# A third group of block 2 turned by VectorE, the last chunk's store in halves, and a new instruction order

## The chip, the cores and the metric

The kernel runs on one core of one Trainium2 chip. Its time is the device time of one execution in microseconds; the median over several runs is compared.

## The reference

Attention with a local window and block summaries, followed by a two-layer block with the gate h * cos(h):

```python
# q, k, v: (4, 8, 768, 64); block 32, window 16; w_in (512, 2048), w_out (2048, 512)
k_sum = k.reshape(B, H, nb, 32, D).max(axis=3)        # 24 block summaries per head
v_sum = v.reshape(B, H, nb, 32, D).mean(axis=3)
scores_l = where(|i - j| < 16, q @ k.T / sqrt(D), -1e9)
scores_s = q @ k_sum.T / sqrt(D) + log(32)
a = softmax(concat([scores_l, scores_s]))             # with + 1e-9 in the denominator
x = (a @ concat([v, v_sum])) -> (3072 tokens, 512)
h = x @ w_in
out = (h * cos(h)) @ w_out
```

The weights arrive as 64-bit floats, the rest as 32-bit floats, and the result is 32-bit.

## The kernel before

The 3072 tokens are eight blocks of 384 (two per batch). In a block, attention works in four **groups** a to d, one for each pair of heads; a name such as b2 is group b (the second pair) of block 2. A group has six tiles of 64 queries. Each tile sees 96 keys and 24 summaries, so its probabilities are 120 wide, padded to 128 with one column for the 1e-9.

The steps of a group, by their names in the order list: `q`, `k`, `v`, `m` load queries, keys, values and the value summaries (one line each on SP's queue of DMAs); `tq`, `tk` turn q and k by TensorE (lines 502, 515) and `cq`, `ck` copy the turned tiles out of PSUM; `ks` takes the block maxima of k (VectorE, line 536); `sc` are the scores (TensorE, line 569); `z` scales and masks (line 580); `mx`, `su`, `ex`, `sm`, `iv`, `nm` are the maximum (VectorE), its subtraction (GpSimd), exp (ScalarE), the sums (VectorE), their inverse (VectorE) and the normalization (GpSimd, line 617); `tp` and `cp` turn the probabilities by TensorE and copy them out; `va` multiplies with the values (TensorE, line 670); `xh` and `xl` split the result into a high and a low part (fp32r).

There is a second way to turn. Two strings of 32 digits, one digit per group, choose it: `TURNS = (q and k, probabilities)`. With a 1, q and k are loaded as 32x32 squares (four DMAs each, line 450, where the other way has two, line 456), and VectorE turns 32x32 elements at once (`qt` line 520, `kt` line 525, straight into the place where TensorE reads them). The probabilities are turned by VectorE too (`pt`, line 640), then written to DRAM (`po`, line 648) and fetched back in four DMAs in another order of the squares (`pi`, line 655), because a transpose of squares leaves the squares where they were. Before the change the groups c2, d2 and all of the blocks 3 to 7 are turned that way, and the blocks 0 and 1 and the groups a2 and b2 by TensorE.

The two-layer part goes in 128 **steps** s0 to s127: for one block and one of 16 slices of 128 of the hidden width, `up` is 12 matmuls of 128x384 (line 714: x high and low with the weight's high, x high with its low part), then `tu`, `re`, `si`, `sq`, `ga` make h * cos(h) by ScalarE and VectorE in turn (lines 724 to 739), `hi` and `lo` split it, and `dh`, `dl` are 6 and 3 matmuls of 128x512 (line 770) into three accumulators, one per chunk of 128 tokens. At the end of a block `ta` takes the three chunks out of PSUM with the sign turned (line 803 on ScalarE, 805 on VectorE) and `st` stores them (line 810). The blocks come in this order: the first six slices of block 0 with part results put away, all of block 1, the rest of block 0, then the blocks 2 to 7.

The **slices** of the weights, w0 to w15, are converted once from 64 bits: `l` loads 1 MB in two DMAs, `ab` (ScalarE), `cl`, `sh`, `lb`, `fb` (VectorE, lines 393, 399, 407, 415) put the bits together, and `hi`, `lo` split into high and low part. The **value summaries** v0_0, v0_1 and so on are loaded (`l`), halved (`h`) and summed (`s`).

All engines run in program order, and that order is written out by hand: the string ORDER is a list of 2247 tokens `who.what.arguments`, where digits are PSUM banks or staging buffers and a last letter the engine (a ScalarE, v VectorE, p GpSimd). The kernel is built by walking the list, so on each engine and on SP's queue the instructions stand as in the list; semaphores order the engines against each other. An instruction that waits holds all that stands behind it on its engine, a DMA on SP's queue too.

Of the kernel before, what the change touches and what calls it, by code (L numbers as in the profile page):

```python
# [20 lines left out]
TURNS = ("00000000001111111111111111111111", "00000000001111111111111111111111")  # L21
# [6 lines left out]
b0.k a0.q a0.k c0.q d0.k b0.tk.0.0 c0.k b0.ck.0.a a0.tq.1 b0.tk.1.2 a0.cq.a v0_1.l b0.ks.1 a0.tk.0.3 b0.ks.0 v0_0.l  # L28
a0.tk.1.4 a0.ck.0.a a0.ks.0 a0.ms.5.6 a0.ck.1.a a0.ks.1 b0.q a0.sc a0.z.1.a a0.z.0.v w1.l a0.mx c0.tk.0.7 a0.su
d0.tk.0.1 c0.ck.0.a d0.tk.1.0 d0.q d0.ks.0 c0.tk.1.3 d0.ck.0.a c0.tq.4 c0.ks.0 c0.ck.1.a c0.ms.6.5 v0_1.h.p d0.ks.1  # L30
c0.cq.a d0.ck.1.v a0.ex w0.l c0.ks.1 c0.sc v0_0.h.v c1.q b0.tq.1 c0.z.1.a b0.ms.7.4 a0.sm b0.ck.1.a v0_0.s.p b0.cq.a
v0_1.s.v c0.z.0.a b0.sc a0.v w1.ab.0 c0.mx w2.l d0.tq.0 b0.z.1.a d0.ms.3.5 w1.cl c0.su b0.z.0.a a0.iv d0.cq.a
w1.sh.6.7 d0.sc a0.nm c0.ex w1.lb c0.m d0.z.0.a d0.z.1.a a0.tp.0.2 w1.fb.1 w0.ab.0 a0.tp.1.1 a0.m d0.mx a0.cp.1.a w5.l
a0.cp.0.a w0.cl d0.su w1.hi.a c0.sm c0.v w0.sh.4.5 w1.lo.p d0.ex d0.m w0.lb w2.ab.0 a0.va.0 c0.iv b1.q w2.cl c0.nm
w0.fb.1 w3.l w2.sh.6.7 w0.hi.a c0.tp.0.3 c0.tp.1.1 a0.xh.a a1.m w0.lo.p d0.sm c0.cp.1.a w5.ab.0 w2.lb d1.m b1.tq.2
c0.cp.0.a d0.iv w5.cl d0.nm c0.va.1 a1.q w2.fb.1 w4.l w5.sh.4.5 w2.hi.a d0.tp.0.3 d0.tp.1.6 d0.v c0.xh.a w2.lo.p b0.mx
w3.ab.0 w5.lb c1.m a1.tq.7 d0.cp.1.a d0.cp.0.a c0.xl b0.su d1.q a1.cq.a a1.ms.6.3 w5.fb.1 b0.ex a1.sc w3.cl d1.v
w5.hi.a b0.sm c1.tq.1 b1.cq.a w3.sh.4.5 w5.lo.p d0.va.7 b0.m a1.z.0.a a1.z.1.a c1.ms.2.6 b0.iv w3.lb d0.xh.a c1.v
w4.ab.0 b0.nm a0.xl c1.cq.a b0.v a1.mx c1.sc w4.cl a1.su a1.v b0.tp.0.3 d0.xl c1.z.0.a w4.sh.0.1 b0.tp.1.7 c1.z.1.a
# [3 lines left out]
w8.sh.6.7 c1.nm a1.va.2 w10.l s1.re w3.hi.a c1.tp.0.0 d1.z.0.v w8.lb c1.tp.1.4 d1.z.1.a w3.lo.p s0.sq s2.up.5 s1.si
d1.mx c1.cp.0.a s0.ga s1.sq d1.su a1.xh.v s0.hi.a s3.up.0 w8.fb.0 c1.cp.1.a w9.ab.1 s0.lo.p s1.ga s2.tu c1.va.3 w9.cl
d1.ex s1.hi.v a2.tq.4 w8.hi.v s1.lo.p s0.dh.6.7.1 b2.q s2.re a1.xl w6.l w8.lo.p s0.dl s3.tu a2.cq.v s2.si d1.sm s1.dh
b2.v s3.re s1.dl d1.iv c1.xh.v d1.nm s3.si s4.up.4 s2.sq c1.xl s3.sq s2.ga w7.ab.0 w9.sh.2.3 d1.tp.0.5 s2.hi.a w7.cl
b1.ex s2.dh s2.lo.p s3.ga w9.lb v1_0.s.p d1.tp.1.0 s4.tu b1.sm d1.cp.1.a s3.hi.a s4.re s5.up.0 v1_1.l d1.cp.0.a b1.iv
w9.fb.1 b1.nm s4.si w7.sh.2.3 s3.lo.p d1.va.5 s4.sq s2.dl w9.hi.v s5.tu s3.dh d1.xh.a s4.ga w9.lo.p w10.ab.0 d1.xl
s5.re b1.tp.0.4 w7.lb s5.si b1.tp.1.5 s3.dl s4.hi.a v1_1.s.p s5.sq s4.dh w7.fb.1 b1.cp.0.a b1.cp.1.a s5.ga w7.hi.a
b1.va.4 v1_2.l s4.lo.v w12.l w10.cl s5.hi.a s4.dl w7.lo.p b1.xh.a s5.dh b1.xl w10.sh.2.3 s6.up.5 w10.lb v1_2.s.p  # L50
w10.fb.0 s7.up.0 s6.tu w6.ab.1 s5.lo.p v1_3.l s6.re w10.hi.v s5.dl s7.tu w6.cl w10.lo.p s8.up.4 s6.si s7.re s5.ta.1.a
s7.si s5.st.1 v1_3.s.v s6.sq s9.up.7 s7.sq s6.ga s5.ta.2.a v1_4.l s7.ga s6.hi.a w6.sh.2.3 s7.hi.a s6.lo.p s10.up.5
s5.ta.0.a s7.lo.p s8.tu s5.st.0 w6.lb w12.ab.0 s5.st.2 v1_4.s.p s6.dh.1.0.6 s8.re w6.fb.1 s8.si s8.sq s6.dl v1_5.l
s8.ga w6.hi.a s7.dh w11.l w12.cl s9.tu w6.lo.p a2.v s7.dl s8.hi.a s9.re s11.up.4 w12.sh.2.3 s9.si s9.sq b2.m s9.ga
s8.lo.p w12.lb s12.up.7 a2.m v1_5.s.p s10.tu s9.hi.a s10.re w12.fb.0 s10.si s8.dh w11.ab.1 s9.lo.p v1_6.l w15.l
w12.hi.a w11.cl s8.dl s9.dh w11.sh.2.3 s10.sq w12.lo.p s11.tu s10.ga s9.dl s11.re s10.hi.a s13.up.5 w11.lb s11.si
s10.lo.p s11.sq v1_6.s.p s11.ga s12.tu s10.dh w11.fb.0 s11.hi.a w15.ab.1 s12.re s10.dl w13.l w15.cl s12.si s14.up.4
# [126 lines left out]
def tile_kernel(  # L184
# [177 lines left out]
    class Slice:  # L362
# [27 lines left out]
        def clamp(self):  # L390

            uf = self.u.bitcast(F32)
            nc.vector.tensor_scalar(out=uf, in0=uf, scalar1=W_LO, scalar2=W_HI, op0=ALU.max, op1=ALU.min)
# [308 lines left out]
    class Step:  # L702
# [88 lines left out]
        def take(self, i, *args):  # L791
# [142 lines left out]
```

## Time and profile before

| | |
|---|---|
| median of 3 runs | 661.95 us (660.78 to 662.87) |
| the profiled execution | 662.1 us |
| its span, first to last instruction | 660.2 us |
| TensorE matmuls busy | 633.9 us, 96% of the span |
| VectorE busy | 451.1 us, 68% |
| ScalarE busy | 366.2 us, 55% |
| GpSimd busy | 214.6 us, 33% |
| DMA | 72.68 MB, mean 110 GB/s |
| mean granted TensorE clock | 0.987 |

The span is the profiler's time from the first to the last instruction; the execution's time has 1.9 us more around it. A busy engine may still be off the path that sets the end. PEld is TensorE's weight load, which overlaps its matmuls. SPq rows are the times at which SP's queue issues a DMA, not the transfer itself.

### The profile page before, as it was taken

How to read it: one execution, taken by the hardware profiler on the slowest of the kernel's cores; microseconds unless marked ns; L12 is line 12 of the kernel's file. 1: busy time of each engine (PE TensorE's matmuls, PEld its weight loads, DVE VectorE, ACT ScalarE, POOL GpSimd, SP SyncE). 2: the span in 40 equal slices, each digit the busy share in tenths (PEclk: the TensorE clock that was granted, in tenths of full speed). 3: DMA queues.
4: the chain of work that ended last, by engine and by line, in shares of the span. 5: the costliest groups of instructions: out<-in, count | busy, mean ns of one | idle time of the engine just before them, and what ended most of it. 6: DMA issues, size and time to landing. Idle time of an engine off the chain costs nothing.

```text
span 660.2 us, 13296 instructions
## 1 busy us (share of the span) xinstructions
PE 633.9 (96%) x5150; PEld 561.5 (85%) x5150; DVE 451.1 (68%) x792; ACT 366.2 (55%) x645; POOL 214.6 (33%) x217
## 2 busy tenths in 40 slices
PE   6569999999999999999999999999999999999997
PEld 4347889889888989898988988989898988989996
DVE  3998998988656676658786667577686564534433
ACT  3666968776663375546575663335545554443443
POOL 4674777754220242302333340012332132010001
PEclk9879999999999999999999999999999999999999
DMA  9898725443331443434553544423243424000001
GB/s 229 260 268 224 239 94 176 160 111 59 69 108 52 128 127 105 115 71 98 123 156 78 150 125 132 92 54 81 85 120 104 104 91 115 0 1 17 32 1 48
DMA packets 164647, 72.68 MB, mean 110 GB/s; under 512 B 134441, under 2 KB 153193, under 8 KB 164585
## 3 DMA queue, kind: packets, MB, share of 16 engines
q1 hardware_dynamic: 164584, 71.84, 40.6%
q8 instruction: 40, 0.66, 0.4%
q14 instruction: 23, 0.18, 0.1%
HBM read 53.72 MB, written 15.73 MB: 105 GB/s over the span
## 4 chain that ended last, share of the span: by engine, by line
PE 87%; SPq 4%; DMA 4%; ACT 2%; issue 1%; DVE 1%; POOL 1%; ACTq 0%
PE banks L770 40%; PE banks L714 39%; PE banks L569 4%; PE banks L670 3%; DMA late<-in_moe_w_out_dram 3%; SPq L456 1%; SPq L493 1%; SPq L477 1%; ACT stage L388 1%; ACT L732 0%; POOL w L356 0%; SPq L485 0%; PE banks L626 0%; ACT w L350 0%; SPq L254 0%
## 5 line engine op out<-in xcount | busy, mean ns | idle before, releaser
L714 PE MATMUL banks<-xh,w 128*128 128x384 f32 x1024 | 271.8, 337 | 1.1 <-ACT pt L350 0.7
L770 PE MATMUL banks<-w,gh 128*128 128x512 f32 x768 | 199.1, 394 | 0.0
L714 PEld LDWEIGHTS banks<-xh,w 128*128 128x128 f32 x1024 | 185.9, 188 | 3.9 <-ACT pt L350 0.9
L714 PE MATMUL banks<-xl,w 128*128 128x384 f32 x512 | 171.4, 335 | 0.0
L770 PEld LDWEIGHTS banks<-w,gh 128*128 128x128 f32 x768 | 142.0, 188 | 29.0
L356 POOL TENSOR_TENSOR gl<-t,gh 128x384 fp32r<-128x384 f32 x57 | 58.5, 1027 | 242.9 <-DVE gh L352 86.0
L724 ACT ACTIVATE t<-banks 128x384 int32<-128x384 f32 x128 | 62.2, 489 | 131.1 <-DVE gl L356 56.1
L727 DVE SCALAR_TENSOR_TENSOR t<-t,banks 128x384 f32<-128x384 int32 x128 | 69.5, 547 | 61.2 <-ACT t L724 60.7
L770 PE MATMUL banks<-w,gl 128*128 128x512 f32 x384 | 109.6, 393 | 0.0
L739 DVE SCALAR_TENSOR_TENSOR t<-t,banks 128x384 f32<-128x384 f32 x128 | 69.8, 547 | 45.4 <-ACT t L735 44.9
L732 ACT ACTIVATE t<-t 128x384 f32<-128x384 f32 x128 | 66.3, 523 | 60.1 <-DVE t L727 59.4
L714 PEld LDWEIGHTS banks<-xl,w 128*128 128x128 f32 x512 | 96.1, 188 | 1.7
L770 PEld LDWEIGHTS banks<-w,gl 128*128 128x128 f32 x384 | 71.3, 188 | 14.8 <-POOL gl L356 0.2
L593 POOL TENSOR_TENSOR sc<-sc,m 128x720 f32<-128x720 f32 x28 | 39.5, 1410 | 88.9 <-DVE m L588 83.8
L735 ACT ACTIVATE t<-t 128x384 f32<-128x384 f32 x128 | 65.9, 522 | 2.4
L617 POOL TENSOR_TENSOR sc<-sc,r 128x720 f32<-128x720 f32 x28 | 39.6, 1416 | 73.1 <-DVE r L614 70.2
L350 ACT CAST gh<-t 128x384 fp32r<-128x384 f32 x71 | 36.2, 510 | 41.3 <-PE banks L770 21.8
L356 DVE TENSOR_TENSOR gl<-t,gh 128x384 fp32r<-128x384 f32 x71 | 40.6, 573 | 19.6 <-PE banks L770 12.0
L356 POOL TENSOR_TENSOR w<-stage,w 128x1024 fp32r<-128x1024 f32 x15 | 36.7, 2448 | 14.7 <-ACT w L350 12.8
L569 PEld LDWEIGHTS banks<-kd,qd 64*64 64x64 f32 x1344 | 27.8, 133 | 9.6 <-issue 5.3
L580 DVE SCALAR_TENSOR_TENSOR sc<-banks,mask 128x360 f32<-128x360 f32 x48 | 24.7, 523 | 16.5 <-PE banks L569 16.3
L569 PE MATMUL banks<-kd,qd 64*64 64x96 f32 (+1 forms) x1344 | 30.9, 231 | 0.6 <-ACT qd L508 0.4
(100 smaller groups left out, 606.8 us busy)
## 6 DMA issues: line engine op xcount, KB each, us to landing
pd<-stage SPq DMA_DIRECT2D x22, 384.0 KB
late<-in_moe_w_in_dram SPq DMA_DIRECT2D x16, 512.0 KB
late<-in_moe_w_out_dram SPq DMA_DIRECT2D x16, 512.0 KB
pt<-pd SPq DMA_DIRECT2D x66, 96.0 KB
vn<-in_v_dram SPq DMA_DIRECT2D x52, 120.0 KB
out_dram<-stage SPq DMA_DIRECT2D x23, 256.0 KB
kn<-in_v_dram SPq DMA_DIRECT2D x24, 192.0 KB
qn<-in_q_dram SPq DMA_DIRECT2D x88, 48.0 KB
```

The source lines that it names most:

```text
L350: eng.copy(out=out, in_=in_)
L356: eng.tensor_tensor(out=lo, in0=src, in1=hi.bitcast(F32), op=ALU.subtract)
L569: nc.tensor.matmul(out=self.sp[hh][s * QT : (s + 1) * QT, c, lo : lo + n], lhsT=self.qd[rows, t * QT : (t + 1) * QT], rhs=self.kd[rows, ke ...
L593: nc.gpsimd.tensor_tensor(out=self.sc, in0=self.sc, in1=self.m.unsqueeze(2).broadcast_to([P, U, NK]), op=ALU.subtract)
L617: nc.gpsimd.tensor_tensor(out=self.sc, in0=self.sc, in1=self.r.unsqueeze(2).broadcast_to([P, U, NK]), op=ALU.mult)
L714: nc.tensor.matmul(out=self.h, lhsT=w_of(name, self.f)[:, c * P : (c + 1) * P], rhs=x_of(self.blk, part, c), start=n == 0, stop=n == last,)
L724: nc.scalar.activation(out=self.t.bitcast(I32), in_=self.h, func=AF.Copy, scale=1.0 / TWO_PI)
L727: nc.vector.scalar_tensor_tensor(out=self.t, in0=self.t.bitcast(I32), scalar=-TWO_PI, in1=self.h, op0=ALU.mult, op1=ALU.add)
L732: nc.scalar.activation(out=self.t, in_=self.t, func=AF.Sin, scale=0.5)
L735: nc.scalar.activation(out=self.t, in_=self.t, func=AF.Square, scale=math.sqrt(2.0))
L739: nc.vector.scalar_tensor_tensor(out=self.t, in0=self.t, scalar=-1.0, in1=self.h, op0=ALU.add, op1=ALU.mult)
L770: nc.tensor.matmul(out=self.acc[i], lhsT=g[:, i * P : (i + 1) * P], rhs=w_of(name, self.f), start=self.first and n == 0, stop=self.last an ...
```

## The change

`TURNS` gets a 1 for b2 in both strings, so b2 is turned by VectorE as c2 and d2 are: its q and k come in squares, its `tq`, `cq`, `tk`, `ck`, `tp`, `cp` go, and `qt`, `kt`, `pt`, `po`, `pi` come. The clamp of a weight slice (`cl`) can go to GpSimd too, and does for w3 and w7. The last chunk of the last step is taken out of PSUM in two halves of 256 columns, the first by ScalarE (`ta`), the second by VectorE (`tb`), and stored by two DMAs (`st`, `sb`). The whole order list is written anew (2245 tokens, different from the first token on), with other banks and staging buffers and with some operations on another engine.

```diff
-TURNS = ("00000000001111111111111111111111", "00000000001111111111111111111111")
+TURNS = ("00000000011111111111111111111111", "00000000011111111111111111111111")
...
-b0.k a0.q a0.k c0.q d0.k b0.tk.0.0 c0.k b0.ck.0.a a0.tq.1 b0.tk.1.2 a0.cq.a v0_1.l b0.ks.1 a0.tk.0.3 b0.ks.0 v0_0.l
+a0.q b0.k a0.k c0.k a0.tq.0 d0.k c0.q b0.tk.0.1 b0.tk.1.2 b0.ck.0.v v0_0.l b0.ks.0 a0.tk.0.3 a0.tk.1.4 a0.ck.0.a
...
-s127.lo.p s127.dh s127.dl s127.ta.1.1.a s127.ta.0.0.v s127.ta.2.a s127.st.1 s127.st.2 s127.st.0
...
+s127.si s127.sq s127.dl s127.ga s126.dh s127.hi.a s127.lo.p s126.dl s127.dh s127.dl s127.ta.2.a s127.ta.1.1.v
+s127.st.2 s127.ta.0.0.v s127.st.1 s127.tb.2.v s127.st.0 s127.sb.2
...
-        def clamp(self):
+        def clamp(self, eng):
...
-            nc.vector.tensor_scalar(out=uf, in0=uf, scalar1=W_LO, scalar2=W_HI, op0=ALU.max, op1=ALU.min)
+            eng.tensor_scalar(out=uf, in0=uf, scalar1=W_LO, scalar2=W_HI, op0=ALU.max, op1=ALU.min)
...
+        def negative(self, eng, to, from_):
+            if eng is nc.scalar:
+                eng.mul(out=to, in_=from_, mul=-1.0)
+            else:
+                eng.tensor_scalar_mul(to, from_, -1.0)
+
+        def take_half(self, i, h, eng):
+            if (i, 0) not in self.o:
+                t = xp.tile([P, 2, TB], F32R, name="last", tag="xh0%d" % (self.blk % 2)).rearrange("p c n -> p (c n)")
+                self.o[i, 0], self.o[i, 1] = (t[:, n * DM // 2 : (n + 1) * DM // 2].bitcast(F32) for n in range(2))
+            self.negative(eng, self.o[i, h], self.acc[i][:, h * DM // 2 : (h + 1) * DM // 2])
...
+        def store_half(self, i, h):
+            r0, c = self.blk * TB + i * P, slice(h * DM // 2, (h + 1) * DM // 2)
+            nc.sync.dma_start(out=out[r0 : r0 + P, c], in_=self.o[i, h])
```

In the new list's front, v0_1's halving is on VectorE instead of GpSimd, b0's first and a0's second half of turned keys are copied by VectorE and d0's second by ScalarE, `a0.iv` stands ahead of `w1.cl`, `w4.lb` and `a1.sm` stand behind `b0.xl`, SP's queue has d0.v and b0.v ahead of w4's load and further forward, and a0.v behind c0.m and a0.m. Where b2 is turned, the list reads:

```text
b2.kt.0 s18.si a2.iv w14.lo.v a2.nm s17.dl b2.kt.1 s20.up.5 s18.sq b2.qt c2.k s19.tu s18.ga b2.ks.0 s18.hi.a
a2.tp.0.2 b2.ks.1 s18.lo.p c2.q b2.sc.3.0
...
b2.pt.0 s21.ta.0.1.a b2.po d2.sc.7.3
...
s22.dh.4.7.3 s23.lo.p s24.re a2.xl b2.pi d2.su s25.tu
...
c2.sm s22.dl s24.si s23.dh c2.iv s25.re c2.nm s28.up.6 s24.sq s25.si s24.ga s24.hi.a s24.lo.v b2.va.0
```

More of the change, by code (lines that the diff above doesn't have):

```diff
@@ L43 @@
[L43 to L47, printed above, removed]
@@ L893, in tile_kernel @@
             up="up", tu="turns", re="residue", si="sine", sq="square", ga="gate", hi="high_part",
[L894 removed]
+            lo="low_part", dh="down", dl="down_low", fe="fetch", ad="add", ta="take", tb="take_rest", st="store",
+            sb="store_rest",
         ),
```

306 lines of the change are left out of this document (157 added, 149 removed).

## Prediction

> **What bounds the kernel now.** I read the page's busy times and slices first, then the busy times by stretch, then who waits for whom. The page:
>
> ```profile
> PE 633.9 (96%) x5150; PEld 561.5 (85%) x5150; DVE 451.1 (68%) x792; ACT 366.2 (55%) x645; POOL 214.6 (33%) x217
> PE   6569999999999999999999999999999999999997
> ```
>
> TensorE is busy for 633.9 of 660.2 us, and its gaps lie in the first slices and the last. The stretches show where (columns: stretch, its length, busy us and instruction counts of PE, PEld, DVE, ACT and POOL, granted clock, DMA share, GB/s):
>
> ```profile
> 20.00:30.00 10.00, 4.01 (x82) 2.82 (x75) 9.50 (x11) 6.89 (x11) 5.44 (x7) 0.91 0.89 259
> 30.00:40.00 10.00, 5.06 (x53) 4.20 (x55) 9.89 (x13) 5.18 (x7) 8.96 (x5) 0.50 0.90 265
> 40.00:50.00 10.00, 6.86 (x99) 5.25 (x96) 9.64 (x13) 6.97 (x12) 7.11 (x5) 0.84 0.88 231
> 60.00:80.00 20.00, 19.12 (x184) 16.65 (x183) 18.05 (x29) 17.68 (x30) 12.73 (x9) 1.00 0.86 269
> 140.00:180.00 40.00, 40.00 (x411) 36.25 (x406) 31.59 (x54) 26.72 (x47) 17.52 (x13) 1.00 0.31 58
> ```
>
> There are three stages. From 20 to 50 us VectorE is nearly full (9.50, 9.89, 9.64 of 10), the DMA engines carry about 0.9, and TensorE is half idle. From about 100 us TensorE has no gap (nines in all slices but the last, 40.00 of 40 from 140 to 180). At the end, stores alone remain. So a matmul taken away after 100 us is worth its own time, an engine that gets faster there is worth nothing, and in the front what counts is when VectorE and the loads deliver. TensorE's waits, in us, times, longest:
>
> ```profile
> PE banks L670 <- ACT late L606: 4.9, 1, 4.9
> PE banks L670 <- DMA x<-in_v_dram: 2.2, 1, 2.2
> PE banks L626 <- POOL late L617: 2.2, 2, 1.7
> PE banks L714 <- ACT pt L350: 0.7, 1, 0.7
> ```
>
> **Term 1: b2's turns leave TensorE, -1.6 us.** b2 loses 15 transposes by TensorE: three for q, six for k, six for the probabilities. Their cost is the time from their first start to the start of the next matmul:
>
> ```profile
> 140.58 0.55 PE L502 MATMUL banks<-ident,qn 128*128 128x128 f32 x3
> 140.88 0.48 PE L770 MATMUL banks<-w,gh 128*128 128x512 f32 x1
> ...
> 146.52 0.82 PE L515 MATMUL banks<-ident,kn 128*128 128x128 f32 x6
> 147.10 0.48 PE L770 MATMUL banks<-w,gl 128*128 128x512 f32 x1
> ...
> 174.72 0.82 PE L626 MATMUL banks<-ident,sc 128*120 128x128 f32 x6
> 175.47 1.09 PE L569 MATMUL banks<-kd,qd 64*64 64x96 f32 x48
> ```
>
> That is 0.30 + 0.58 + 0.75 = 1.63 us, all inside the stretch without gaps. In their place VectorE gets one q, two k and one probability transpose:
>
> ```profile
> L640 DVE STREAM_TRANSPOSE stage<-sc 128x768 f32<-128x768 f32 x22 | 21.4, 973 | 7.8 <-POOL sc L617 6.9 <-DMA out_dram<-stage 0.9
> L525 DVE STREAM_TRANSPOSE kd<-kn 128x384 f32<-128x384 f32 x20 | 11.4, 569 | 0.0
> ```
>
> q and each half of k are 128x384, so 3 x 0.57 + 0.97 = 2.7 us, in a stretch in which it is idle for 40 - 31.59 = 8.4 us. I cost it at nothing. If that cover were gone, the step residues and gates behind them on VectorE would be 2.7 us late, and a later up would hold TensorE by at most that. ScalarE loses five copies out of PSUM less one that VectorE did.
>
> On SP's queue b2's loads become four of q and four of k where there were two of each, and the probabilities go out and come back through DRAM. The same things as other groups issue them:
>
> ```profile
> 155.72 2.02 SPq L450 DMA_DIRECT2D kn<-in_k_dram  x4
> 161.60 1.85 SPq L450 DMA_DIRECT2D qn<-in_q_dram  x4
> 185.70 0.34 SPq L648 DMA_DIRECT2D pd<-stage  x1
> 188.40 1.72 SPq L655 DMA_DIRECT2D pt<-pd  x4
> ```
>
> That is 2.0 + 1.9 + 0.3 + 1.7 = 5.9 us of issue, less some 2 us that the old loads took. SP has room, since the DMA share is 0.31. From the store at 185.70 to the end of the fetches' issue at 190.1 are 4.4 us. In the new order 87 matmuls stand between b2.po and b2.va (one group's scores, two ups, two downs less one low part); at 40.00 us for 411 from 140 to 180 these are 8.5 us, so the way through DRAM is covered. c2.k, which needs the one key buffer that b2.kt.1 frees, stands 72 matmuls or 7 us ahead of c2.kt.0 and takes 2.0 us to issue.
>
> [...]
>
> **Term 2: the new order in the front, -1.6 us.** I multiplied VectorE's instructions in both order lists by the mean durations below and compared what stands ahead of the first step's matmuls (s0.up, at 58.27 us, which waits for b0.xl).
>
> ```profile
> L407 DVE SCALAR_TENSOR_TENSOR banks<-late,banks 128x1024 int32<-128x1024 int32 x16 | 19.6, 1224 | 0.2
> L393 DVE TENSOR_SCALAR stage<-stage 128x1024 f32<-128x1024 f32 x16 | 12.9, 809 | 4.3 <-ACT stage L388 4.1
> L609 DVE TENSOR_REDUCE r<-sc 128x6 f32<-128x726 f32 x28 | 25.0, 896 | 3.3 <-ACT sc L606 3.1
> ...
> 17.16 1.38 DVE L259 TENSOR_TENSOR late<-late 96x1024 f32<-96x1024 f32 x1 [1.16 <-DMA late<-in_v_dram]
> 22.61 1.65 DVE L393 TENSOR_SCALAR stage<-stage 128x1024 f32<-128x1024 f32 x1 [0.37 <-ACT stage L388]
> 57.57 0.56 DVE L356 TENSOR_TENSOR xl<-banks,xh 128x384 fp32r<-128x384 f32 x1
> ...
> 58.27 0.43 PE L714 MATMUL banks<-xh,w 128*128 128x384 f32 x1
> ```
>
> Ahead of w1.cl (22.61) the new list gives VectorE one halving of v more (1.38), net one copy (0.55, by L356's row) and a0.iv (a reciprocal of 128x6, some 0.2 as the smallest of all here): 2.1 us. VectorE waits 1.16 + 0.37 us there, so some 0.6 us of it shows. Between w1.cl and b0.xl (57.57) the lists differ by four instructions that are no longer there: w3.cl (0.81, now POOL's), w4.lb (1.22) and a1.sm (0.90), now behind, and a0.iv (0.2), now ahead: 3.1 us. VectorE is full there, so b0.xl could come 3.1 - 0.6 = 2.5 us sooner. The moved work comes due later: up to s6.up five instructions have left (a0.iv 0.2, w3.cl and w7.cl 0.8 each, one copy 0.55, one weight cast of about 1.0, between the rows of 0.81 and 1.22 for its size) and three have come (two casts of a step, some 0.4 each, as 3/8 of the weight cast's elements, and w10.lb, 1.22): 3.3 - 2.0 - 0.6 leaves 0.7 us sooner. TensorE then runs no further ahead than VectorE allows, so the gain lies between 0.7 and 2.5, and I take the middle, 1.6.
>
> The loads must let it. In the old order d0.v stood behind w4's 1 MB and landed for 48.33, where TensorE had waited 2.2 us (the L670 row above); now it stands ahead of w4. b0.v too is five loads further ahead. Against that, a0.v now comes last of its group on SP, behind c0.m and a0.m:
>
> ```profile
> 31.65 1.67 PE L670 MATMUL banks<-pt,vn 120*64 120x64 f32 x24 [4.89 <-ACT late L606]
> ```
>
> Its three DMAs at some 0.5 us of issue each (0.46, a quarter of L450's 1.85 for four) are 1.5 us, so a0.va, which starts at 31.65, may start some 1.6 us later. The next group of probabilities on TensorE waits 1.7 us anyway (longest of POOL late L617), which hides it. If this cover is gone and VectorE gains nothing, the front is 1.6 us later. Ends of this term: -2.5 and +1.6.
>
> **Term 3: the last chunk in halves, +0.4 us.** The end now:
>
> ```profile
> 655.18 0.69 DVE L805 TENSOR_SCALAR stage<-banks 128x512 f32<-128x512 f32 x1 [2.07 <-PE banks L770]
> 655.40 0.60 ACT L803 ACTIVATE stage<-banks 128x512 f32<-128x512 f32 x1 [3.35 <-PE banks L770]
> 655.66 0.39 PE L770 MATMUL banks<-w,gl 128*128 128x512 f32 x1
> 656.03 0.33 SPq L810 DMA_DIRECT2D out_dram<-stage  x1
> 656.08 0.60 ACT L803 ACTIVATE last<-banks 128x512 f32<-128x512 f32 x1
> 656.71 0.33 SPq L810 DMA_DIRECT2D out_dram<-last  x1
> 657.13 0.41 SPq L810 DMA_DIRECT2D out_dram<-stage  x1
> ...
> 657.00:658.00 1.00, 0.00 (x0) 0.00 (x0) 0.00 (x0) 0.00 (x0) 0.00 (x0) 1.00 1.04 389
> 658.00:659.00 1.00, 0.00 (x0) 0.00 (x0) 0.00 (x0) 0.00 (x0) 0.00 (x0) 1.00 0.91 350
> ```
>
> ScalarE's half ends at about 656.08 + 0.4 = 656.48 (between 0.60 for the whole and 0.30 for half of it). On SP this half now stands first, so the other two stores, the first of which was ready at 656.03, wait for it: SP starts 0.45 us later. On VectorE chunks 1 and 0 take 2 x 0.69 from 655.40, to 656.78, and the second half some 0.4 more, to 657.2; SP, with four issues of 0.33 to 0.41, starts its last at about 657.6 where it was 657.13, +0.5. The DMA engines are full from 657 to 659 (1.04, 0.91), so the same bytes started 0.45 us later end that much later. A last store of half the bytes gives back up to half of 256 KB at 389 GB/s, 0.3 us. So +0.15 to +0.5; I take 0.4. Below nothing, -0.3, only if the fewer bytes count in full and the later start not at all.
>
> **The sum.** -1.6 - 1.6 + 0.4 = -2.8 us. The profiled execution took 662.1 us (660.2 of span, 1.9 around it), 0.15 above the median of the runs, 661.95. So the profiled time becomes 659.3 and the median 659.15, say 659.2. The rest of the new order I cost at nothing: after 100 us TensorE waits for nobody, and the mean number of other steps' matmuls between a step's up and its down, counted in the two lists from step 6 on, grows from 64 to 70, so the steps keep a little more reserve.
>
> **The rivals.** *The front gives everything back*: VectorE's 0.7 us by s6.up is small, and a wait of TensorE for w3 or the conversions after it eats it. For it speaks that VectorE is nearly full at 60 to 80 us too (18.05 of 20); against it, that TensorE waits so little there (0.7 for ACT pt). Then 661.95 - 1.6 + 0.4 = 660.75.
>
> *The half clock spreads, slower than before.* The clock is at 0.50 from 30 to 40 us, after a stretch in which TensorE did 4.01 of 10 us. If a0.va's wait of 4.9 us grows by the 1.6 of a0.v, the clock may stay down through the next stretch as well. The 6.86 busy us of 40 to 50 would then take up to twice as long; half of that, 3.4 us, I count, because part of it already runs at less than full clock (0.84). With the 1.6: 661.95 - 1.6 + 0.4 + 3.4 + 1.6 = 665.75. It decides where TensorE does no more than some 5 of 10 us from 40 to 50 as well. Against it stands the shorter wait for d0.v. [...]
>
> *The turned group holds TensorE, so that the saving doesn't show.* b2.sc stands right behind b2.ks.1 with no matmul between. So it did before (b2.ks.0) and TensorE did not wait, but the new order has three transposes of 0.57 us packed ahead of it. TensorE waiting there for as long as it saves, with the front's gain: 661.95 - 1.6 + 0.4 = 660.75.
>
> **The chances.** The forecast 0.60 (own range 657.6 to 661), the front given back 0.18, the half clock 0.13, the held group 0.09. A measurement tells 0.3%, 2.0 us, from no change, so faster means below 659.96: three quarters of the forecast's 0.60, 0.45, and a little of the others. The two middle rivals and the rest of the forecast are no change: 0.40. Slower has the half clock and a little more: 0.15. The range goes from 656.8 (front -2.5, tail -0.3, and half a microsecond for the unknown) to 663.2, with the slower case beyond it.
>
> **What would show it.** Right: TensorE instructions fall by 15 transposes and nothing is idle on it from 100 us on; s0.up starts between 55.8 and 57.6; no wait for x<-in_v_dram; the last store starts on SP at some 1.6 us after the last matmul's end. Wrong: a gap on TensorE before b2.sc or b2.va (term 1), a first up at 58 or later or new waits after it (term 2), a longer stretch at half clock, or an end that is closer to the last matmul than now, 4.1 us (term 3).

## The result, and the profile after

The changed kernel takes 667.85 us (median of 6 runs, 665.03 to 670.15) against 662.41 before (6 runs, 660.78 to 663.10). The ratio is 1.0073, 95% interval 1.0051 to 1.0096. It is slower by some 5 us; I had forecast 659.2 us, and the range to 663.2 doesn't hold it. The profiled execution took 668.58 us (span 666.6). Its page, busy times and slices of TensorE and its granted clock:

```profile
PE 632.9 (95%) x5135; PEld 559.8 (84%) x5135; DVE 445.7 (67%) x778; ACT 370.4 (56%) x651; POOL 225.1 (34%) x235
PE   6469799899999999999999999999999999999997
PEclk9879999899999999999999999999999999999999
```

The 15 transposes are gone (5150 to 5135). New are a seven in the fifth slice of TensorE (67 to 83 us) and an eight in the eighth, for TensorE and for the clock (117 to 133 us). The stretches behind the first up, of the kernel before and then of the changed one (columns as in the prediction):

```profile
58.00:100.00 42.00, 40.43 (x334) 35.19 (x333) 39.38 (x57) 33.86 (x57) 29.77 (x27) 1.00 0.60 191
100.00:130.00 30.00, 30.00 (x155) 27.49 (x154) 26.82 (x37) 23.47 (x42) 22.39 (x26) 1.00 0.54 173
130.00:655.00 525.00, 525.00 (x4134) 470.94 (x4134) 339.16 (x642) 276.13 (x493) 127.82 (x112) 1.00 0.34 86
```

```profile
58.00:100.00 42.00, 37.15 (x310) 31.20 (x309) 36.84 (x51) 33.15 (x53) 31.17 (x25) 1.00 0.58 185
100.00:130.00 30.00, 27.80 (x132) 24.51 (x132) 26.58 (x34) 20.46 (x36) 19.27 (x23) 0.94 0.57 176
130.00:660.00 530.00, 530.00 (x4152) 475.05 (x4151) 334.89 (x632) 285.21 (x508) 137.99 (x135) 1.00 0.34 87
```

From 130 us on TensorE is busy without a gap in both. Before that its idle time rises from 1.57 to 4.85 us (58 to 100) and from 0 to 2.20 us (100 to 130), and the clock of 0.94 over 30 us loses some 1.8 us. VectorE did less from 58 to 100 than before (36.84 against 39.38 us): it wasn't fuller, it stood.

The first matmuls of s0.up and s6.up, before and then after:

```profile
58.27 0.43 PE L714 MATMUL banks<-xh,w 128*128 128x384 f32 x1
...
94.28 0.33 PE L714 MATMUL banks<-xh,w 128*128 128x384 f32 x1
```

```profile
56.67 0.42 PE L714 MATMUL banks<-xh,w 128*128 128x384 f32 x1
...
96.85 0.33 PE L714 MATMUL banks<-xh,w 128*128 128x384 f32 x1
```

So the front gained 1.6 us, as forecast, and by s6.up 2.6 us were lost, where 0.7 should have been kept. Two waits of TensorE carry most of it. The first, with its chain on SP (L371 and L375 are a weight slice's two loads, L456 q, L477 and L485 v), ScalarE and VectorE:

```profile
60.36 1.57 SPq L456 DMA_DIRECT2D qn<-in_q_dram  x2
...
64.59 1.74 SPq L485 DMA_DIRECT2D late<-in_v_dram  x1
66.44 0.39 SPq L371 DMA_DIRECT2D late<-in_moe_w_in_dram  x1
66.87 0.50 SPq L375 DMA_DIRECT2D late<-in_moe_w_out_dram  x1
67.47 0.38 SPq L371 DMA_DIRECT2D late<-in_moe_w_in_dram  x1
...
74.40 1.12 ACT L388 ACTIVATE stage<-late 128x1024 f32<-128x1024 f32 x1 [3.87 <-DMA late<-in_moe_w_out_dram]
75.56 1.03 DVE L393 TENSOR_SCALAR stage<-stage 128x1024 f32<-128x1024 f32 x1 [2.94 <-ACT stage L388]
78.04 0.45 PE L714 MATMUL banks<-xh,w 128*128 128x384 f32 x1 [3.02 <-DVE qd L352]
```

The load of slice w9 (67.47 us) now stands behind a2's q, a1's and d1's v and w6. Its first instruction w9.ab holds ScalarE for 3.87 us, w9.cl holds VectorE for 2.94, and behind w9.cl stands a2.cq, which empties the PSUM bank that s4.up takes next. Before, the same load and w9.ab were at

```profile
63.78 0.39 SPq L371 DMA_DIRECT2D late<-in_moe_w_in_dram  x1
...
71.51 1.14 ACT L388 ACTIVATE stage<-late 128x1024 f32<-128x1024 f32 x1 [0.74 <-DMA late<-in_moe_w_out_dram]
```

The second wait is s10.dh's, behind w11.ab on ScalarE, and a half clock comes after it:

```profile
119.15 1.14 ACT L388 ACTIVATE stage<-late 128x1024 f32<-128x1024 f32 x1 [1.58 <-POOL gl L356]
123.38 1.87 PE L770 MATMUL banks<-w,gh 128*128 128x512 f32 x6 [1.92 <-ACT gh L350]
...
122.00:124.00 2.00, 0.62 (x3) 0.54 (x4) 2.00 (x4) 1.17 (x4) 2.00 (x2) 1.00 1.03 379
124.00:126.00 2.00, 2.00 (x8) 1.56 (x7) 1.99 (x4) 1.20 (x3) 1.84 (x4) 0.66 1.12 314
126.00:128.00 2.00, 2.00 (x8) 1.90 (x7) 1.75 (x4) 1.96 (x3) 0.56 (x2) 0.50 0.45 87
```

The account: the last matmul ends at 661.68 us instead of 656.05, 5.6 later. Two landmarks divide this, the first matmul of s0.up and that of s14.up. Between them both kernels run the same matmuls, and from s14.up on the same but for b2's 15 transposes (the counts take in one to three more, which a stretch's edges cut). Before, and then after:

```profile
58.27:122.19 63.92, 62.35 (x445) 55.23 (x444) 58.46 (x81) 50.79 (x87) 46.48 (x45) 1.00 0.59 187
122.19:655.66 533.47, 533.47 (x4177) 478.67 (x4175) 347.11 (x653) 282.65 (x504) 133.50 (x118) 1.00 0.34 86
```

```profile
56.67:129.20 72.53, 65.48 (x445) 56.24 (x444) 63.94 (x86) 53.94 (x89) 50.22 (x48) 0.98 0.58 181
129.20:661.29 532.09, 532.09 (x4161) 476.92 (x4161) 335.94 (x633) 285.70 (x509) 138.79 (x135) 1.00 0.34 87
```

So 1.6 us are won ahead of s0.up, 8.6 (72.53 - 63.92) lost from there to s14.up, and 1.4 (533.47 - 532.09) won behind it. Of the 8.6, idle time (3.3 + 2.2) and clock (1.8) make 7.3; the other 1.3 us lie in time in which TensorE counts as busy, and I couldn't place them. The end adds 0.8:

```profile
661.29 0.39 PE L770 MATMUL banks<-w,gl 128*128 128x512 f32 x1
661.72 0.38 ACT L806 ACTIVATE last<-banks 128x256 f32<-128x256 f32 x1 [3.68 <-PE banks L770]
662.13 0.33 SPq L830 DMA_DIRECT2D out_dram<-last  x1
662.25 0.41 DVE L808 TENSOR_SCALAR last<-banks 128x256 f32<-128x256 f32 x1
662.55 0.88 SPq L826 DMA_DIRECT2D out_dram<-stage  x2
663.53 0.40 SPq L830 DMA_DIRECT2D out_dram<-last  x1
...
663.00:664.00 1.00, 0.00 (x0) 0.00 (x0) 0.00 (x0) 0.00 (x0) 0.00 (x0) 0.97 0.91 331
664.00:665.00 1.00, 0.00 (x0) 0.00 (x0) 0.00 (x0) 0.00 (x0) 0.00 (x0) 0.50 1.00 370
```

### The profile page after: what moved, and what is told of

Read it like the earlier page. It is cut to its first block, busy times and chain, and to the rows that moved or that the text cites. A ratio compares the mean times of both kernels' runs of the same rounds, so it can differ in the third digit from the quotient of the medians.

```text
span 666.6 us, 13262 instructions
## 1 busy us (share of the span) xinstructions
PE 632.9 (95%) x5135; PEld 559.8 (84%) x5135; DVE 445.7 (67%) x778; ACT 370.4 (56%) x651; POOL 225.1 (34%) x235
## 4 chain that ended last, share of the span: by engine, by line
PE 83%; DMA 5%; DVE 4%; ACT 2%; SPq 2%; issue 2%; POOL 1%; DVEq 0%; ACTq 0%
PE banks L770 38%; PE banks L714 37%; DMA late<-in_moe_w_out_dram 5%; PE banks L569 4%; PE banks L670 3%; DVE banks L399 1%; ACT stage L388 1%; SPq L456 1%; PE banks L515 1%; SPq L371 1%; POOL late L259 0%; DVE stage L393 0%; DMA late<-in_k_dram 0%; POOL stage L393 0%; DVE t L727 0%
## 5 line engine op out<-in xcount | busy, mean ns | idle before, releaser
L356 POOL TENSOR_TENSOR gl<-t,gh 128x384 fp32r<-128x384 f32 x56 | 56.8, 1015 | 224.2 <-DVE gh L352 101.6
L739 DVE SCALAR_TENSOR_TENSOR t<-t,banks 128x384 f32<-128x384 f32 x128 | 69.0, 546 | 61.8 <-ACT t L735 61.6
L350 ACT CAST gh<-t 128x384 fp32r<-128x384 f32 x74 | 37.7, 510 | 51.3 <-DVE t L739 27.1
L356 DVE TENSOR_TENSOR gl<-t,gh 128x384 fp32r<-128x384 f32 x72 | 43.7, 608 | 24.4 <-PE banks L770 15.5
L356 POOL TENSOR_TENSOR w<-stage,w 128x1024 fp32r<-128x1024 f32 x14 | 33.4, 2389 | 9.3 <-ACT w L350 9.3
```

The costliest lines, as they stand in the source:

```text
L350: eng.copy(out=out, in_=in_)
L356: eng.tensor_tensor(out=lo, in0=src, in1=hi.bitcast(F32), op=ALU.subtract)
L739: nc.vector.scalar_tensor_tensor(out=self.t, in0=self.t, scalar=-1.0, in1=self.h, op0=ALU.add, op1=ALU.mult)
```

## The experiments

Every run stands beside runs of the kernel before on the same chip (medians 662.0 to 662.9 us). "Seam" is an order that follows one list up to a token and the other list behind it, with the PSUM banks renamed so that no live bank is overwritten. A ratio is not the quotient of the two medians and can differ from it (for s10_first that quotient is 1.0064).

| run | median us (runs) | ratio to before, 95% interval |
|---|---|---|
| after_again (the changed kernel once more) | 667.60 (6) | 1.0066, 1.0044 to 1.0088 |
| old_58: old order to s0.up, then new | 667.49 (5) | 1.0065, 1.0052 to 1.0079 |
| old_100: old order to b1.xl, then new | 663.67 (12) | 1.0004, 0.9991 to 1.0016 |
| old_front: old order to s14.dh, then new | 662.86 (12) | 1.0006, 0.9990 to 1.0021 |
| old_front_whole: and last chunk whole | 661.38 (12) | 0.9996, 0.9980 to 1.0011 |
| old_128: seam at s13.re, last chunk whole | 662.31 (12) | 0.9985, 0.9969 to 1.0001 |
| new_front: new order to 145 us, the rest as before | 668.17 (6) | 1.0087, 1.0058 to 1.0116 |
| new_start: new to s0.up, old to s14.dh, new; whole | 662.59 (12) | 0.9996, 0.9984 to 1.0007 |
| w9_early | 665.49 (6) | 1.0049, 1.0035 to 1.0063 |
| cq_first | 667.57 (5) | 1.0080, 1.0067 to 1.0092 |
| s10_first | 666.59 (6) | 1.0078, 1.0058 to 1.0099 |
| both | 666.45 (12) | 1.0058, 1.0041 to 1.0075 |
| stalls_mended | 664.79 (12) | 1.0030, 1.0012 to 1.0047 |
| best_try | 664.33 (12) | 1.0035, 1.0018 to 1.0052 |
| b2_mended: before, b2's turns alone | 663.04 (12) | 0.9997, 0.9982 to 1.0013 |
| three_stalls: before, three chains later | 662.96 (12) | 1.0004, 0.9990 to 1.0018 |
| late_values: before, three stalls | 687.31 (5) | 1.0390, 1.0365 to 1.0414 |

### Where the loss is: seams

```diff
-ORDER = new list
+ORDER = old list up to s14.dh + what is left of the new list   # old_front
+last chunk: ta.1 ta.0 ta.2 st.1 st.2 st.0, whole               # old_front_whole
+ORDER = new list up to a2.mx + what is left of the old list    # new_front, b2 not turned, chunk whole
+ORDER = old list up to s0.up (old_58) or b1.xl (old_100) + the rest of the new list
```

> The changed kernel with the order of the kernel before up to s14.dh (about 135 us, 524 of its entries) and the new order behind it, PSUM banks renamed so that the two parts fit; b2 is turned by VectorE and the last chunk goes in halves. Theory (all that the change lost is lost by the new order ahead of 130 us, in waits and a half-clock window; the rest of it costs nothing): kernel before minus 1.6 us for b2's turns plus 0.8 us for the halves, 661.6 us, TensorE 100% busy from 130 us on. Rival (the new order behind 130 us loses part of it, or b2's turns cost what they save): 663 to 668 us.

> As the run with the old front, and the last chunk taken and stored whole, in the order of the kernel before (ta.1, ta.0, ta.2, st.1, st.2, st.0). If the halves cost 0.8 us (end of the last matmul to the end of the span 4.9 us in the changed kernel against 4.15 before): 0.8 us below it, 660.8 us, which would beat both kernels. Rival (the distance at the end is the storm of stores by chance of the DMA queues): within 0.3 us of it.

> The opposite mix: the new order up to about 145 us (a2's scores), the old order behind it, b2 turned by TensorE as before, the last chunk whole. Theory (the new order of the front alone carries the loss): the changed kernel's 667.85 plus 1.6 minus 0.8 us, 668.7 us, 6 us slower than the kernel before. Rival (the loss lies in the rest or in the mixture of both): 661 to 664 us.

> The changed kernel with the order of the kernel before up to s0.up alone (about 58 us) and the new order from there, banks renamed to fit; b2 turned, halves at the end. If all of the loss (old front 662.86, changed kernel 667.85: 5.0 us) lies between s0.up and 135 us, and the new order ahead of s0.up gains 1.6 us as the profile of the changed kernel says: 667.85 + 1.6 = 669.5 us. If the loss lies ahead of s0.up in most executions, and the profiled one was a good one: about 663 us. In between, each part has its share.

> As the run with the old order up to 58 us, with the seam at b1.xl (about 100 us). Theory: the w9 and s4 place (75 to 82 us, 3.2 to 4 us) lies ahead of the seam and is cured, the s10 place (121 to 128 us, 3.6 us) behind it. If that place loses by itself: 662.86 + 3.6 = 666.5 us. If it was only the lateness passed on from the first: 662.9 us, within 1 us of the old front.

The place is settled. With the old order up to 100 us the kernel is as fast as before (1.0004); with the old order up to s0.up alone it is as slow as the changed one (1.0065); the new front with all of the old rest is slow too (1.0087). So the loss of 0.6%, 4 us, lies between s0.up and b1.xl, from 58 to 100 us. Two of these runs missed what was expected of them: old_front stands 1.3 us above its 661.6, and old_58 2.0 us below its 669.5, which took the new start to be worth 1.6 us in most executions. old_100 still has the s10 wait,

```profile
120.05 1.65 PE L770 MATMUL banks<-w,gh 128*128 128x512 f32 x6 [1.30 <-ACT gh L350]
```

and is not slower than old_front for it: the s10 place, with 3.6 us in the first profile, isn't where the kernels differ in most executions.

### What makes it: the late slice

```diff
# w9_early (SP)
-... d1.v a1.tp.1.1 ... w6.l ... w9.l
+... w9.l d1.v a1.tp.1.1 ... w6.l ...
# cq_first (VectorE)
-w9.cl.v ... s2.re ... a2.cq.v
+a2.cq.v w9.cl.v ... s2.re ...
# s10_first (ScalarE, VectorE)
-w11.ab.0 ... w12.hi.a w11.cl.v ... s10.sq ... s11.tu s10.ga ... s10.hi.a
+w12.hi.a s10.sq w11.ab.0 ... s10.ga w11.cl.v ... s10.hi.a s11.tu
# both = w9_early + s10_first
```

> The changed kernel (667.85 us) with one weight slice's load, w9.l, issued on SP ahead of d1.v, w6.l instead of behind them: issue at about 63.7 us instead of 67.5. Theory A (the 3.0 us for which s4.up waits for its bank are owed to w9's late landing, through w9.ab on ACT and w9.cl on VectorE, behind which the copy a2.cq that empties the bank stands): w9.ab starts at 71 to 72 us instead of 74.4, s4.up's wait of 3.02 us goes, the median falls by 3 us, to 664.9, and by a little more if what is late behind it (s10's wait at 121 us) gets shorter too. Rival (the bank was asked for too early by the order of TensorE, the load is an accident of the same place): the wait stays above 1.5 us, the median falls by less than 1 us. Second rival (another load on SP, d1.v or w6.l, is then late in its turn): a new wait of TensorE for a tile of d1.va or a later conversion, median 666 to 668.

> The changed kernel with one VectorE instruction moved: a2.cq (empties PSUM bank 5, 0.5 us) ahead of w9.cl, which waits for w9's load; the load stays where it is. Theory A': what TensorE stood for is only the place of a2.cq behind the stalled w9.cl; then s4.up's wait of 3.02 us goes though w9.ab still starts at 74.4 us, and the median falls by up to 3 us, to about 665. Rival: the whole of ACT and VectorE behind w9.ab and w9.cl is late (s2.tu, s2.re, s1.lo), so TensorE stands a little later for another of them, a wait of 2 to 3 us at s1.dl, s2.dh or s4's neighbours between 76 and 82 us, and the median falls by less than 1 us.

> The changed kernel with s10's chain put ahead of a weight slice's conversion at 118 to 123 us: on ACT w12.hi and s10.sq ahead of w11.ab, s10.hi ahead of s11.tu; on VectorE s10.ga ahead of w11.cl. Theory B (s10.dh's wait of 1.92 us at 121.5 us is owed to w11.ab, which waits for its load at the head of ACT, and the half clock of 3.4 us from 124.7 us on follows that idle time): s10.hi starts by 121.3 us instead of 122.8, the wait goes, no half-clock window after it, and the median falls by 1.9 + 1.7 = 3.6 us, to about 664.2. Rival (the clock window comes anyway, whatever TensorE did before it): the median falls by 1.9 us only, to about 666, and a slice near 125 us still shows a clock near 0.5. Second rival (w11's conversion is then late for s11 in its turn): s11.dh waits 1 to 2 us, median 666 to 668.

> The changed kernel with both moves, w9.l early and s10's chain ahead of w11.ab. If theories A and B are both right the gains add: 3.0 + 3.6 us, median about 661.2, within 0.3% of the kernel before. If B's wait is only A's lateness passed on, this run equals the one with w9.l alone within 1 us.

In w9_early the load, w9.ab and the next wait of TensorE are

```profile
63.42 0.38 SPq L371 DMA_DIRECT2D late<-in_moe_w_in_dram  x1
...
70.13 1.15 ACT L388 ACTIVATE stage<-late 128x1024 f32<-128x1024 f32 x1 [0.44 <-DMA late<-in_moe_w_out_dram]
...
81.47 0.43 PE L626 MATMUL banks<-ident,late 128*120 128x128 f32 x2 [1.59 <-DVE t L739]
```

The wait for s4's bank is gone, and the median is 2.4 us lower (2.1 against after_again; by the ratios 1.1 to 1.6). Another of 1.59 us for a bank came some 3 us later, which may be why less than 3.0 was won. cq_first shows that the place of the one copy is not the cause: s4.up no longer waits, but the whole of ScalarE and VectorE is still behind w9, TensorE waits for others, and the time stays (1.0080):

```profile
81.43 0.65 PE L626 MATMUL banks<-ident,late 128*120 128x128 f32 x4 [3.57 <-POOL late L617]
83.80 0.68 PE L626 MATMUL banks<-ident,late 128*120 128x128 f32 x2 [1.71 <-DVE t L739]
```

So theory A' falls, and theory A stands as to the wait. But an earlier load alone is not enough. In the profile of s10_first, which leaves this place as it was, w9's load happens to be issued at 64.43 us, 3.0 earlier than in the first profile, and w9.ab starts at 72.31, 2.1 earlier; s4.up still waits 3.10 us. There w9.cl stands 2.88 us beside GpSimd's w8.lo (the two rows in the last section). In w9_early w9.cl runs from 72.28 to 72.96, ahead of w8.lo at 73.80. That w9.cl has to come ahead of w8.lo is read from these profiles; no run moves w8.lo.

s10_first takes the s10 wait (0.29 us is the longest there in its profile, instead of 1.92), but by its ratio gains nothing (1.0078; its median is 1.0 to 1.3 us lower, so a small gain is open). In its profile another wait, of 0.70 us, came at 128.00, and from s14.up to the last matmul it takes 533.17 us, where eight profiles with the new order there have 532.09 to 532.13. Theory B, that this place is worth 3.6 us, falls, as old_100 says too. The run with both moves isn't better than w9_early.

```diff
# stalls_mended = both, and
-d1.tp.0.4 w9.lb d1.tp.1.6 s2.dh
+d1.tp.0.4 w9.lb s2.dh d1.tp.1.6
+last chunk whole
```

> The changed kernel with every stall mended that the profiles of the runs with the new front name: w9.l early on SP, s10's chain ahead of w11.ab, d1.tp.1 behind s2.dh on TensorE (it waited 1.56 us for a PSUM bank in the run with both moves), and the last chunk whole. Theory (the loss is these stalls and the half-clock windows that follow them; what the new order gains at its start is real): the 17.4 us that TensorE lost behind s0.up in the profile with both moves falls by 1.6 and by a window of 1.7, to about 14, the start stays 2 us earlier than before, b2's turns are 1.6 us less: 659 to 660.5 us, faster than the kernel before. Rival (the new order keeps ACT and VectorE so late between 60 and 100 us that another wait comes in the place of each one mended): 662 to 666 us.

1.0030: of the 0.7% some 0.4% are won back, 0.1% of it by the whole chunk. The theory holds in direction and the rival in part: TensorE in this profile waits 1.22 us for a1's probabilities at 61.6 us, then 0.44, 0.52 and 0.70 us, none for the reasons mended. What is left between 58 and 100 us is not one wait, and I can't name it further.

### The terms by themselves

> The kernel before with only b2's turns moved to VectorE: b2.kt and b2.qt stand where TensorE's turns stood, b2.va with the copies behind it and d2's loads of v some 5 us later in the order, because the probabilities go out to DRAM and back. (The run b2_alone let c2's q, k and d2's v be loaded over b2's before these were used; its work isn't that of the kernel.) Theory (term 1): 662.0 - 1.6 = 660.4 us. Rival (VectorE, now with two q and k turns of 0.9 us in the place of 0.5 us copies, passes lateness on, or b2's loads in four pieces are late): TensorE waits before b2.sc or b2.va, 661.5 to 664 us.

> The kernel before with only b2's turns moved to VectorE (its q, k and probabilities; b2.va and the copies behind it some 5 us later in the order, because the probabilities now go out to DRAM and back). Theory (term 1): 15 TensorE transposes less, 1.6 us off the 662.4 us of the kernel before, 660.8 us. Rival (b2's scores or values come late and TensorE waits): 661.5 to 664 us with a gap before b2.sc or b2.va.

(b2_alone, 666.45 us, is the run of which the first of these two speaks; nothing follows from its time.) b2 alone is worth -0.2 us, between -1.2 and +0.9; my 1.6 lies outside. From s14.up to the last matmul its profile has 533.09 us, 0.4 less than before, where the changed kernel has 1.4 less. (A turn of q or of half of k takes 0.57 us in the traces, not the 0.9 that I expected here.) Its profile has a wait inside b2's scores, the only one behind 130 us:

```profile
151.35 0.38 PE L568 MATMUL banks<-kd,qd 64*64 64x96 f32 x2
152.35 1.08 PE L568 MATMUL banks<-kd,qd 64*64 64x24 f32 x46 [0.62 <-DVE kd L535]
```

From the first of these two rows to the second is 1.0 us for two matmuls: the last of VectorE's reductions (L535) was late, and most of the saving went there. The new list has the turns further ahead, and there this wait doesn't come.

```diff
# old_128: seam at s13.re instead of s14.dh, last chunk whole
# new_start: new list to s0.up, old list to s14.dh, new list; last chunk whole
# best_try: new_start with seam at s13.re, and
-d1.v a1.v ... w7.l ... w9.l ... a2.q ... a2.tq.1 ... b2.q ... a2.cq.v     (to 77 us)
+a1.v ... w9.l d1.v w7.l ... a2.q ... (20 us later) a2.tq b2.q ... a2.cq.v
```

> As the run with the old front and the last chunk whole (661.38 us), with the seam at s13.re (about 128 us) instead of s14.dh, banks renamed to fit; at the other seam a2.sc waited 0.76 us. If that wait is all that the seam cost: 660.6 us, 0.2% below the kernel before. Rival (the wait moves on to s13's or s14's products): 661.4 us again.

> The new order up to s0.up (about 57 us), the order of the kernel before from there to s14.dh, the new order behind it, b2 turned, the last chunk whole. Theory (the start gains the 1.6 us that the profile of the changed kernel shows, the middle alone loses): 661.38 - 1.6 = 659.8 us, faster than the kernel before by 0.3%. Rival (the old middle does not fit the new start, or the start gains nothing in most executions): 661 to 664 us.

> The run with the new start and the old middle, with the three waits mended that its profile and that of the old front name: w9.l ahead of d1.v and w7.l on SP (w9.ab had waited 3.62 us for it), a2.tq and a2.cq some 20 us later (a2.tq had waited 1.90 us for a2.q's DMA, and a half-clock window of 3.4 us came behind), the seam to the new order at s13.re instead of s14.dh, the last chunk whole. Theory: 662.59 - 1.9 - 1.7 - 0.8 = 658 to 660 us, faster than the kernel before by 0.3 to 0.6%. Rival (what the new start gains is given back on the way to s5 whatever is mended, since ACT and VectorE aren't earlier with the weights): 661.5 to 663 us.

old_128 is the fastest in ratio, 0.9985 with 1.0001 as its upper end: b2's turns seem to show, but no version here beats the kernel before beyond doubt. The new start is earlier: the profiles with the old order up to s0.up start it at 57.47 to 59.75 us (nine, mean 58.7), those with the new one at 55.64 to 58.38 (ten, mean 57.1). But new_start is no faster than old_front_whole (0.9996 both): with the new start in front of the old order, a2's q comes late,

```profile
74.64 0.55 PE L502 MATMUL banks<-ident,qn 128*128 128x128 f32 x3 [1.90 <-DMA qn<-in_q_dram]
```

and a half clock follows. best_try took that wait and the one for w9 away and is slower (1.0035): b2.q, which I had to move too, waits on SP for a2.tq and holds the value summaries' load behind it, GpSimd waits for these, and s5.dl for GpSimd:

```profile
100.83 1.08 PE L770 MATMUL banks<-w,gl 128*128 128x512 f32 x3 [2.92 <-POOL gl L356]
```

It is my own example of the fault studied: a load moved on SP is paid by whoever stands behind its consumer.

### What a stall costs: the clock

> The changed kernel once more, for a second profile and for more executions beside the runs of this call. If the spread of its times (665.0 to 670.2) comes from half-clock windows behind its two stalls, which come in some executions and not in others, the second profile again shows the waits of about 3 us for s4.up's bank and 1 to 2 us at s10.dh, and windows of 3.4 or 6.8 us at another place or of another number than the first (one, at 124.6 us); time and stalls plus half the windows' length move together, within 0.5 us. Rival (the stalls themselves vary from run to run): no wait of 3 us, a time near 665.

> The kernel before with TensorE made to wait three times where it never waits: the activation of s46 and s78 (turns, residue, sine, square, gate, high and low part) and of s118 (from the sine on) stands directly ahead of the step's first product, so that TensorE waits for the chain, 2 to 4 us at about 254 and 415 us and 1 to 3 us at 613 us. Theory (a stall of TensorE is followed by a half-clock window in part of the cases): time rises by the sum of the stalls plus 1.7 us for each window of 3.4 us, and the profile shows the windows within 10 us behind a stall, and none elsewhere after 60 us. Rival (the windows have nothing to do with idle time): time rises by the sum of the stalls alone, no window behind them.

> The kernel before with three waits put on TensorE where it never waits: the turn of the probabilities, the store to DRAM and the loads back (pt, po, pi) of c3, d5 and c7 stand directly ahead of the group's values, so that c3.va, d5.va and c7.va wait for the way through DRAM, 2 to 6 us each. Theory (a stall of TensorE of 2 us or more is followed by a half-clock window in most cases): the time rises by the sum of the three stalls and by 1.7 us for every window of 3.4 us, which the profile shows within 10 us behind a stall. Rival (the windows at 75 to 125 us in the runs so far have another cause): the time rises by the stalls alone.

```diff
# three_stalls: before, for s46, s78 (all of the chain) and s118 (from si on)
-s46.tu ... s46.re ... s46.si ... s46.hi.a s46.lo.v ... s46.dh
+... s46.tu s46.re s46.si s46.sq s46.ga s46.hi.a s46.lo.v s46.dh
# late_values: before, for c3, d5, c7
-c3.pt.0 c3.po ... c3.pi ... c3.va.3
+... c3.pt.0 c3.po c3.pi c3.va.3
```

three_stalls is a miss: no stall came, and the time is the same. Behind 130 us ScalarE and VectorE are so far ahead that a whole chain can be moved to just ahead of its product. late_values gives the stalls: 5.71, 6.69 and 5.05 us. The stretches about the first (it ends at 278.78):

```profile
272.00:274.00 2.00, 1.07 (x7) 0.75 (x5) 0.48 (x2) 0.80 (x2) 0.97 (x1) 1.00 0.75 223
274.00:276.00 2.00, 0.00 (x0) 0.00 (x0) 1.97 (x4) 1.23 (x3) 0.67 (x1) 1.00 0.18 72
276.00:278.00 2.00, 0.00 (x0) 0.00 (x0) 0.87 (x2) 0.23 (x1) 0.32 (x1) 0.65 0.69 183
278.00:280.00 2.00, 1.22 (x23) 1.25 (x24) 0.00 (x0) 0.00 (x0) 0.00 (x0) 0.50 0.00 1
280.00:282.00 2.00, 2.00 (x11) 1.59 (x9) 0.00 (x0) 0.00 (x0) 0.00 (x0) 0.50 0.24 55
282.00:284.00 2.00, 2.00 (x7) 1.55 (x7) 0.36 (x1) 0.00 (x0) 0.00 (x0) 0.64 0.72 206
284.00:286.00 2.00, 2.00 (x13) 2.00 (x12) 0.69 (x1) 0.00 (x0) 0.00 (x0) 1.00 0.09 30
```

The clock goes to half some 3.5 us after TensorE fell idle (at 276.6) and stays there for 6.83 us; behind the other two it is 10.24 and 6.83. Of these windows 4.7, 5.5 and 5.8 us lie behind the stall's end, and half of their 16.0 is 8.0 us. With the stalls' 17.5 that makes 25.5; measured are 687.31 - 662.48 = 24.8 (from s14.up to the last matmul, in the profiles, 558.37 - 533.47 = 24.9). The theory holds here: the stalls cost their length and about half of what the half clock lasted beyond them. The kernel before, with no stalls there, has no half clock in its profile between 60 us and its last matmul (656.05). In the other profiles, waits of 1.3 us or more behind 60 us and the windows that came with them ahead of the last matmul:

| profile | wait, us (its end) | half clock, us (from) |
|---|---|---|
| after | 3.02 (78.0); 1.92 (123.4) | none; 3.41 (124.6) |
| after_again | 3.78 (78.8); 1.58 (123.6) | 3.41 (79.4); none |
| old_58 | 3.80 (79.3) | 6.83 (78.4) |
| new_front | 3.10 (79.4); 1.38 (124.8) | 6.83 (78.6); none |
| cq_first | 3.57 (81.4), 1.71 (83.8) | 6.83 (82.6) |
| s10_first | 3.10 (77.8) | none |
| w9_early | 1.59 (81.5); 1.36 (120.4) | none |
| both | 1.56 (80.0) | 3.41 (80.0) |
| old_100 | 1.30 (120.1) | none |
| new_start | 1.90 (74.6) | 3.41 (75.5) |
| best_try | 2.92 (100.8) | 3.41 (101.5) |

Every wait above 3.5 us has one, of those between 1.5 and 3.1 five of nine (cq_first's second lies inside a window and isn't counted), below that none. So by that account a wait of much the same length costs up to 1.7 or 3.4 us more in one profile (half of 3.41 or 6.83) and nothing in another. The spread of the times doesn't show this: the changed kernel's (665.0 to 670.2) is no wider than that of the kernel before over all runs (659.6 to 664.9), which has no wait of 1.3 us behind 60 us in its profile. And a profile shows one execution each; after_again had its window at 79.4 where the first profile had it at 124.6, and time and stalls plus half windows did not move together as I expected (4.94 + 1.7 at 668.58 us, 5.36 + 1.7 at 667.23); the start differed as well.

## Why the prediction was wrong

**Term 1, b2's turns, -1.6.** Right for the changed kernel, and only a little too large: 15 instructions less, no gap at b2.sc or b2.va, and 1.4 us less from s14.up to the last matmul (532.09 to 532.13 us in eight profiles, 533.47 and 533.55 in two with b2 turned by TensorE and the old order there). The rival of the held group is real elsewhere: in b2_mended, with the old order around it, it takes most of the saving. That VectorE's 2.7 us are covered is true only where the list brings the turns early enough; idle time summed over 40 us (8.4) does not say that it lies ahead of the scores.

**Term 2, the new front, -1.6.** Its first half was right: s0.up starts at 56.67 us, inside 55.8 to 57.6, and no wait for x<-in_v_dram is left. The step that failed is "up to s6.up five instructions have left [...] and three have come [...] leaves 0.7 us sooner", with "TensorE then runs no further ahead than VectorE allows". I summed VectorE's work, as if it were the limit there; VectorE had less of it and did less. It waited, with ScalarE, for a weight slice, and w9.cl then took longer beside GpSimd's w8.lo (1.03 us here, 2.88 in s10_first, 0.69 before). (The 2.6 us lost by s6.up measured from the start of the span are 4.2 measured from s0.up: 36.01 us before, 40.18 after.) I had asked of the loads only whether v's came in time ("the loads must let it") and did not follow the slices w6, w9, w10, w7 on SP behind a2.q, a1.v and d1.v. w9's load is issued 3.7 us later, and w9.ab starts 2.9 us later. Mending this load alone lowered the median by 2.4 us, mending three waits and the last chunk lowered it by 3.1; between 58 and 100 us the new order loses 4 us in all (seams), so part of it has no name. One candidate is untested: I took the clamps of w3 and w7 off VectorE (0.69 us) and gave them no price on GpSimd, where they take 3.62 us each; no run puts them back.

**The rest of the new order, costed at nothing.** Right from s14.up on (no more than b2's term differs there) and, by the medians, about right from 100 us (old_100 and old_front are no slower than before), wrong ahead of it, with the reason just given. "After 100 us TensorE waits for nobody" was read from the old profile; in the new one it waits at s10.dh, which the medians do not show.

**Term 3, the halves, +0.4.** Right in sign, too small. From the last matmul's end to the end of the span nine profiles with halves have 4.92 to 4.95 us, nine with the whole chunk 4.15 to 4.27 and a tenth 4.62 (b2_mended): +0.7. The mis-sized part is the credit of up to 0.3 us for a last store of half the bytes. The last issue starts 1.85 us behind the last matmul's end (663.53 - 661.68; I had 1.6), where it was 1.08, and the DMA engines are full for the same two microseconds behind it (0.91, 1.00), so the later start counts in full.

**The rivals.** The first (a wait for "the conversions after it" eats the front's gain) had the mechanism; I priced it as the gain lost, 660.75, with 0.18. It does not stop at the gain, because a stalled slice holds all of ScalarE and VectorE (w9 for 3.87 and 2.94 us in the profile after) and so is passed on from bank to bank. The half clock came too, not in the front where I put it but behind the new waits, at 1.7 us for a window of 3.41. Both together are the case that I held at 0.13 to 0.15. In that rival a longer wait of a0.va was to keep the clock down; in the profile before, that wait of 4.9 us lasts from 26.76 to 31.65, and the half clock starts inside it, at 28.24. The range was loose too: its low end comes to 661.95 - 1.6 - 2.5 - 0.3 - 0.5 = 657.05, not 656.8, its high end of 663.2 has no sum, and the slower case that I priced at 665.75 lay outside it. I gave 0.45 to faster because each moved instruction made the sum smaller; the sum had no term for a load.

## What to carry to other kernels

When an order list moves, follow each load on its queue to the instruction that waits for it and to everything that stands behind that instruction on its engine, and on to the PSUM banks that these free: the sum of an engine's work says nothing where the engine waits. Price a wait of TensorE in a full stretch with half a clock window on top (here 1.7 us for the 3.41 us that came behind some waits), and compare medians, not one profile, once such waits exist. To find where a rewritten order loses, splice it with the old one at a few seams and time the mixtures; that placed the loss in two runs where the profile's largest two waits had named one right and one wrong place.

## What the runs showed of the hardware

Between 60 us and the last matmul the half clock comes in lengths of 3.41, 6.83 and 10.24 us, and behind waits of 3.1 us there is one in new_front and none in s10_first. Shorter waits differ too: with those of 1.92 us in the changed kernel, 1.90 in new_start and 1.56 in the run with both moves a half clock of 3.41 us came, with those of 1.58 us in after_again and 1.59 in w9_early none. No run here shows what decides it. In the kernel before, the half clock that starts at 28.24 us follows 3.41 us in which TensorE was busy for 0.87.

One clamp of a weight slice took four times as long as another. In s10_first, the clamp and the GpSimd instruction beside it:

```profile
73.43 2.38 POOL L356 TENSOR_TENSOR w<-stage,w 128x1024 fp32r<-128x1024 f32 x1
73.47 2.88 DVE L393 TENSOR_SCALAR stage<-stage 128x1024 f32<-128x1024 f32 x1 [1.10 <-ACT stage L388]
```

The same clamp takes 0.69 us in the kernel before (72.69 us) and 1.03 in the changed one, where such a GpSimd instruction ended 0.48 us after its start. It ends 0.54 us behind GpSimd's here (76.35 and 75.81) and 0.55 us behind it in the changed kernel (76.59 and 76.04), as if it began when that was done. That the one instruction held the other is my reading of these rows; no run shows the cause.
